# Four more products with w_out in three passes, and a new order of all steps

## The chip, the cores and the metric

The kernel runs on one core of a Trainium2 chip. The metric is the time of one execution on the device in microseconds (us), as the median of several runs.

## The reference

Attention with a causal mask feeds two matrix stages. Cut to what matters:

```python
q, k, v: (2, 12, 448, 64)
scores = where(triu, -1e9, (q @ k.T) / 8)
x = softmax(scores) @ v            # as 896 tokens x 768
h = x @ moe_w_in                   # 768 x 2048
x = (maximum(h, 0) ** 2) @ moe_w_out                       # 2048 x 768
h = maximum(maximum(x @ w1, x @ w2), x @ w3)               # 768 x 768 each
out = h @ w_out                    # 896 x 768, float32
```

## The kernel before

All tokens and weights are kept transposed on 128 partitions. The twelve pairs of heads go through attention one by one (`Pair`): score matmuls in plain float32 (step s), the masked minimum on VectorE (m), the exponential on ScalarE (e), the normalizing on GpSimd or VectorE (n), transposes on PE (g), their placing by ScalarE or VectorE (h) and the weighing with v on PE (w).

The four matrix stages each use a fast scheme for 2 x 2 blocks with seven products M1 to M7 in place of eight. `First` is x @ w_in in eight column pairs f0 to f7, `Second` is the product with moe_w_out in eight blocks o0 to o7 of its inner dimension, `Third` is the three products with w1, w2, w3 (h0 to h8), and the code at the end is the product with w_out.

A product is made in three passes over split operands: each operand is split in a rounded part (hi) and the rest (lo), both of a type that PE takes in one pass, and the product is hi*hi + hi*lo + lo*hi. For one product of `First`, `Second` or `Third` that is nine matmuls of 448 columns; in some of them one is cut into two of 224 columns (`matmul_in_parts`). The weights' split is `Quarter`: H.name casts 128x384 on ScalarE, H'.name on GpSimd, and L.name subtracts on VectorE. The result lies in one of five buffers (`RING`), which come free when PE has read them. In `Second` the moving operand is split as well: XH.name on ScalarE, XL.name on VectorE, 128x448 each; it lies in one of a pool of units. Steps S1 to S4 form sums of moving operands on VectorE, T1 to T4 sums of weights in place, T1, T3 and T4 by an accumulating DMA that GpSimd issues. C and J unpack a block of weights on ScalarE and VectorE, V steps carry results out of PSUM.

`FULL` names products of `Second` that are not split: M1 of blocks 0 to 3 go through `run_full`, three matmuls in plain float32 each, straight from the loaded weights and the activations (line 852).

The order of all steps is a table, `ORDER`: the program is written step by step as it stands there, and every engine works through its instructions in that order and waits only for the data and buffers that they need. A quote after a step's letter names the other engine for it. Behind the table a fixed tail follows with the rest of the last stage.

Of the kernel before, what the change touches and what calls it, by code (L numbers as in the profile page):

```python
# [33 lines left out]
h2.1 m0.3 e3.2 s4.3 n3.1 e0.3 a0'.2 m1.3 s2.3 a2.2 a1'.2 r0.2 n6'.2 h0.1 xh.0 g1.1 h1.1 r2.2 m4.3
r1.2 n0'.2 g3.2 s6.3 n5.2 m5.3 m3.3 e4.3 s6.4 n2.2 m2.3 n4.2 n3.2 e5.3 m6.3 h3.2 e1.3 m6.4 wload
n1.2 g0.2 e6.3 a0'.3 g1.2 g2.2 s0.4 xl.0 e2.3 xf'.0 a2'.3 s2.4 m0.4 e3.3 m1.4 s4.4 r0.3 r2.3 m2.4
m3.4 s2.5 e2.4 a1'.3 r1.3 n6.3 n1'.3 n3.3 h0'.2 e3.4 m5.4 m4.4 e6.4 w0.1 w1.1 n4'.3 h2'.2 n2.3
w2.1 h1.2 a1'.4 w3.1 e5.4 e0.4 n0.3 n5.3 g1.3 r1.4 g2.3 g3.3 n3.4 e1.4 e4.4 h2.3 a2'.4 s6.5 h1'.3
g0.3 d3.1 w0.2 m2.5 w1.2 w2.2 e2.5 C.i0 h3.3 a0'.4 w3.2 r0.4 n5.4 m3.5 n2.4 r2.4 s4.5 m6.5 h0.3
# [18 lines left out]
M1b.f0 a1'.11 w0.9 C.i4 n1.10 4l.3 H.f0M6 d4.7 r1.11 n4'.10 w1.9 w2.9 a2.11 w3.9 M1c.f0 r0.11
M2a.f1 r2.11 M2b.f0 4h.7 h3.10 g2.10 h1.10 n5.11 M1b.f1 3l.5 2h.7 g0.10 n4.11 d3.9 n0.11 4l.7
n1'.11 1l.7 h2.10 h0.10 g2.11 T1.f1 n3'.11 g0.11 w0.10 V0.f0M1 h2.11 n6.11 T3.f0 J.i4 w1.10 w2.10  # L60
3h'.9 2l.7 w3.10 T4.f0 xh'.10 xl.10 H'.f0M7 T3.f1 n2.11 C.i5 h0.11 g3.11 g1.11 J.i5 h3.11 h1.11
M1c.f1 xf.10 L.f0M6 M2c.f0 w0.11 w1.11 w2.11 T2.f1 w3.11 M2b.f1 V0.f1M1 T4.f1 C.i7 d2.11 L.f0M7
M2c.f1 2h.11 2l.11 M6.f0 H.f2M2 H.f1M6 d1.11 L.f1M6 xh.11 V0.f0M6 1h'.11 H.f1M7 J.i7 more V0.f1M2
# [1176 lines left out]
```

## Time and profile before

| | us |
|---|---|
| median of three runs | 449.04 (448.46 to 449.26) |
| the profiled execution, its own time | 448.89 |
| its span, first to last instruction | 446.9 |
| PE busy in the span | 441.8 |
| VectorE busy | 392.2 |
| ScalarE busy | 294.8 |
| GpSimd busy | 130.3 |

The clock of TensorE was granted in full throughout (1.00 in every stretch). The span falls into the attention stage (up to about 88 us), `First` (to about 188), `Second` (from 180 to about 294, with `Third` beginning inside its end), `Third` (to about 407) and the rest. The time of the profiled execution is its span and about 2 us around it. PE's own busy share says little, since matmuls overlap each other in the records; more is read from when one group starts after the other.

### The profile page before, as it was taken

Reading aid. Unit: us, or ns where it says so; the run is one execution under the profiler, and the core shown is the slowest. Engines: PE = TensorE matmul, PEld = TensorE weight load, DVE = VectorE, ACT = ScalarE, POOL = GpSimd, SP = SyncE. Lnnn points to the kernel's source line nnn. Section 1 sums busy time; section 2 is a strip of 40 time slices with the busy share of each in tenths; the row PEclk is TensorE's granted clock in tenths of the full one; section 3 lists DMA queues with packets and bytes.
Section 4 is the critical chain, followed back from the end, with each engine's and each line's share of the span. In section 5 each row is a group of like instructions: output and inputs, shape, how many; then the busy total and the mean of one; then the engine's idle time right before and its main releaser. Section 6 shows DMA issues by size and latency. Waiting matters only on the chain.

```text
span 446.9 us, 7146 instructions
## 1 busy us (share of the span) xinstructions
PE 441.8 (99%) x2380; PEld 387.0 (87%) x2380; DVE 392.2 (88%) x847; ACT 294.8 (66%) x657; POOL 130.3 (29%) x212
## 2 busy tenths in 40 slices
PE   8999999999999999999999999999999999999996
PEld 5666667799999999789999999999999999999996
DVE  5899999998987789999999899999897778889963
ACT  5999999766685797977566795656454533542651
POOL 4666575422311112142654312210321012100000
PEclk9999999999999999999999999999999999999999
DMA  7383374456646454899596554304462440000114
GB/s 223 114 266 123 115 240 149 124 170 195 194 113 205 133 151 118 235 181 208 146 168 180 162 160 141 119 24 141 142 211 72 142 132 11 2 0 0 37 53 160
DMA packets 42853, 61.01 MB, mean 137 GB/s; under 512 B 2113, under 2 KB 35009, under 8 KB 42817
## 3 DMA queue, kind: packets, MB, share of 16 engines
q1 hardware_dynamic: 39072, 55.61, 40.2%
q0 software_dynamic: 3456, 4.72, 6.4%
q8 instruction: 19, 0.31, 0.3%
q10 hardware_dynamic: 288, 0.23, 0.2%
q14 instruction: 18, 0.14, 0.1%
HBM read 53.08 MB, written 2.75 MB: 125 GB/s over the span
## 4 chain that ended last, share of the span: by engine, by line
PE 94%; DVE 5%; issue 0%
PE ps L583 69%; PE ps L438 7%; PE ps L480 5%; PE ps L511 5%; PE ps L1027 5%; PE ps L852 2%; DVE piece L200 1%; DVE z L210 1%; DVE wd L210 1%; PE ps L1092 1%; DVE s L210 0%; DVE z2l L200 0%; DVE wol L200 0%; DVE half L200 0%; DVE warm L1087 0%
## 5 line engine op out<-in xcount | busy, mean ns | idle before, releaser
L583 PE MATMUL ps<-s,wq 128*128 128x448 f32 (+1 forms) x629 | 130.1, 361 | 0.0
L583 PEld LDWEIGHTS ps<-s,wq 128*128 128x128 f32 x629 | 115.5, 188 | 9.6 <-issue 0.7
L583 PE MATMUL ps<-a,wq 128*128 128x448 f32 x459 | 99.3, 367 | 0.0
L583 PE MATMUL ps<-x,wq 128*128 128x448 f32 (+1 forms) x481 | 96.5, 362 | 0.0
L583 PEld LDWEIGHTS ps<-x,wq 128*128 128x128 f32 x481 | 88.3, 188 | 7.5 <-issue 0.7
L583 PEld LDWEIGHTS ps<-a,wq 128*128 128x128 f32 x459 | 85.8, 188 | 7.2 <-issue 0.4
L287 POOL CAST wq<-wd 128x384 fp32r<-128x384 f32 x43 | 36.1, 842 | 115.1 <-PE ps L583 97.0
L271 DVE SCALAR_TENSOR_TENSOR wd<-wr,up 128x768 int32<-128x768 int32 x56 | 55.1, 984 | 8.0 <-ACT up L264 4.2
L200 DVE TENSOR_TENSOR wq<-wd,wq 128x384 fp32r<-128x384 f32 x95 | 52.7, 566 | 8.3 <-POOL wq L287 5.2
L261 ACT CAST up<-wr 128x768 f16<-128x768 bf16 x40 | 43.2, 1080 | 12.4 <-DVE wd L271 3.1
L287 POOL CAST wq<-wt 128x384 fp32r<-128x384 f32 x32 | 21.5, 673 | 93.0 <-PE ps L583 74.4
L200 DVE TENSOR_TENSOR wq<-wt,wq 128x384 fp32r<-128x384 f32 x68 | 38.1, 571 | 11.9 <-ACT wq L197 7.7
L457 ACT ACTIVATE pr<-pr,st 128x256 f32<-128x256 f32 (+3 forms) x84 | 43.9, 530 | 3.8 <-DVE st L449 3.2
L197 ACT CAST wq<-wd 128x384 fp32r<-128x384 f32 x52 | 26.7, 513 | 26.0 <-PE ps L583 21.3
L472 POOL TENSOR_SCALAR pr<-pr,st 128x384 f32<-128x384 f32 (+3 forms) x64 | 36.9, 589 | 13.3 <-DVE st L468 11.3
L449 DVE CUSTOM_DVE_ANT_0 pr<-ps,mask 128x128 f32<-128x128 f32 (+3 forms) x84 | 34.7, 442 | 4.8 <-PE ps L438 4.0
L616 ACT COPY s<-ps 128x448 f32<-128x448 f32 x38 | 19.9, 530 | 24.6 <-PE ps L583 24.6
L438 PE MATMUL ps<-k,q 64*128 64x128 f32 (+3 forms) x168 | 34.7, 448 | 0.0
L197 ACT CAST wq<-wt 128x384 fp32r<-128x384 f32 x36 | 18.4, 511 | 15.7 <-PE ps L583 15.3
L480 PEld LDWEIGHTS ps<-ident,pr 128*128 128x128 f32 x192 | 21.3, 141 | 6.2 <-issue 2.8
L480 PE MATMUL ps<-ident,pr 128*128 128x128 f32 x192 | 25.5, 277 | 0.0
L438 PEld LDWEIGHTS ps<-k,q 64*128 64x128 f32 (+1 forms) x168 | 17.8, 196 | 8.7 <-DVE st L449 4.0
(123 smaller groups left out, 642.3 us busy)
## 6 DMA issues: line engine op xcount, KB each, us to landing
wr<-in_moe_w_out SPq DMA_DIRECT2D x22, 768.0 KB, 4.5
wr<-in_moe_w SPq DMA_DIRECT2D x18, 768.0 KB, 4.4
wr<-in_moe_w_in SPq DMA_DIRECT2D x16, 768.0 KB, 4.9
v<-in_v SPq DMA_DIRECT2D x12, 256.0 KB, 4.6
wd<-wd POOLq DMA_DIRECT2D x16, 192.0 KB, 5.5
q<-in_q SPq DMA_DIRECT2D x11, 256.0 KB, 2.6
out<-s SPq DMA_DIRECT2D x14, 192.0 KB, 2.0
k<-in_k SPq DMA_DIRECT2D x11, 224.0 KB, 2.9
```

What stands on the lines that cost most here:

```text
L197: nc.scalar.copy(hi, src)
L200: nc.vector.tensor_tensor(out=lo, in0=src, in1=hi.bitcast(F32), op=SUB)
L261: copy(self.up.bitcast(FH)[:, :, 1::2], self.top)
L271: nc.vector.scalar_tensor_tensor(out=self.t.bitcast(I32), in0=self.rest, scalar=13, in1=self.up.bitcast(I32), op0=ALU.logical_shift_right, ...
L287: copy(self.t[:, 0], self.src())
L438: nc.tensor.matmul(sc[:, :keys[w]], self.n["q"][r, w // 2 * P:(w // 2 + 1) * P], self.n["k"][r, :keys[w]], start=True, stop=True,)
L449: nc.vector.tensor_tensor_reduce(out=self.pr[:, offs[u]:offs[u] + n], in0=self.sc[u][:, :n], in1=mask[:, mask.shape[1] - n:], scale=-SCALE ...
L457: nc.scalar.activation(sl, sl, ACTF.Exp, bias=self.st[:, 0, u:u + 1], scale=-1.0, accum_out=self.st[:, 1, u:u + 1],)
L472: engine.tensor_scalar(sl, sl, self.st[:, 2, u:u + 1], 1.0, op0=ALU.mult, op1=ALU.mult)
L480: nc.tensor.transpose(pt[:, i], self.pr[:, offs[u] + kc * P:offs[u] + (kc + 1) * P], shared["ident"])
L511: nc.tensor.matmul(self.pv[r, kc * P:], self.n["v"][:, kc, r], self.ph[:, h, at], start=kc == 0, stop=kc == NK - 1,)
L583: nc.tensor.matmul(acc[:, c], w, x[:, c], skip_group_check=True, **flags)
```

## The change

`FULL` becomes empty: the four plain products M1.o0 to M1.o3 are split like the others. For each of them four steps come into the table (XH, XL, H or H', L), 16 in all. The table is replaced by one from a new search, so that nearly every engine's order changes in places, and 143 of the old steps stand on another engine than before. The number of casts of weights on GpSimd goes from 78 to 87, on ScalarE from 93 to 88. Nothing else in the code changes.

```diff
-FULL = dict(M1=(0, 1, 2, 3))
+FULL = dict()
...
-s0.0 m0.0 s2.0 m1.0 s4.0 m2.0 e0.0 m3.0 s6.0 e1.0 e3.0 m4.0 m5.0 a2'.0 m6.0 e4.0 r2.0 n1.0 e5.0
+s0.0 m0.0 m1.0 s2.0 e1.0 e0.0 s4.0 m2.0 m3.0 m4.0 e3.0 m5.0 s6.0 s6.1 e4.0 e5.0 a2'.0 m6.0 e6.0
```

On PE at the place of the first plain product, before (ps are PSUM banks, a22 and s4 operands of `First`, g activations, wd loaded weights, wq split weights):

```order
L583 MATMUL ps1_69<-a22_579,wq_1987 128x448 x3
L583 MATMUL ps1_69<-a22_903,wq_1987 128x448 x3
L583 MATMUL ps1_69<-a22_1175,wq_1987 128x448 x3
L852 MATMUL ps6_74<-g0_1244,wd_1764 128x448
L852 MATMUL ps7_75<-g0_1244,wd_1764 128x448
L852 MATMUL ps0_68<-g0_1244,wd_1764 128x448
L583 MATMUL ps4_72<-s4_690,wq_2034 128x448 x3
L583 MATMUL ps4_72<-s4_1035,wq_2034 128x448 x3
L583 MATMUL ps4_72<-s4_1264,wq_2034 128x448 x3
L852 MATMUL ps6_74<-g2_1191,wd_1620 128x448
```

and now (x is a split moving operand):

```order
L585 MATMUL ps1_69<-s3_465,wq_2007 128x448 x3
L585 MATMUL ps1_69<-s3_776,wq_2007 128x448 x3
L585 MATMUL ps1_69<-s3_1198,wq_2007 128x448 x3
L585 MATMUL ps6_74<-x_1559,wq_1963 128x448 x3
L585 MATMUL ps7_75<-x_1559,wq_1963 128x448
L585 MATMUL ps7_75<-x_1559,wq_1963 128x224 x2
L585 MATMUL ps7_75<-x_1559,wq_1963 128x448
L585 MATMUL ps0_68<-x_1559,wq_1963 128x448 x3
L585 MATMUL ps4_72<-s4_803,wq_2035 128x448 x3
L585 MATMUL ps4_72<-s4_1055,wq_2035 128x448 x3
L585 MATMUL ps4_72<-s4_1342,wq_2035 128x448 x3
```

The three plain matmuls of M1.o0 have become nine and one cut in two, from x and wq in place of g0 and wd, and M4.f7 stands behind M1.o2 now and M7.f7 ahead.

On VectorE at the same place, from the last output of `First`'s blocks 6 and 7 on, before:

```order
L210 TENSOR_TENSOR g15_2070<-ps5_73,s_2014 128x448
L271 SCALAR_TENSOR_TENSOR wd_2084<-wr_2028,up_64 128x768
L210 TENSOR_TENSOR s2_2088<-g9_1824,g8_1743 128x448
L210 TENSOR_TENSOR g10_1787<-g10_1787 128x448
L200 TENSOR_TENSOR wq_2094<-wd_1588,wq_2094 128x384
L271 SCALAR_TENSOR_TENSOR wd_2100<-wr_2048,up_64 128x768
L200 TENSOR_TENSOR x_2065<-g8_1743,x_2065 128x448
L200 TENSOR_TENSOR wq_2053<-wd_1661,wq_2053 128x384
L210 TENSOR_TENSOR g13_1999<-ps4_72,s_1889 128x448
L200 TENSOR_TENSOR wq_2067<-wd_1764,wq_2067 128x384
L200 TENSOR_TENSOR wq_2059<-wd_1753,wq_2059 128x384
L210 TENSOR_TENSOR g0_1244<-s2_1900,g0_1244 128x448
```

and now (x_1948 is the operand of M1.o3, wq_1986 and wq_2038 are the weights of M1.o1 and M1.o2; g0 is overwritten by S1 of block 0):

```order
L212 TENSOR_TENSOR g13_2063<-ps4_72,s_2020 128x448
L273 SCALAR_TENSOR_TENSOR wd_2067<-wr_1943,up_64 128x768
L202 TENSOR_TENSOR wq_2035<-wd_1476,wq_2035 128x384
L202 TENSOR_TENSOR x_1948<-g6_1534,x_1948 128x448
L202 TENSOR_TENSOR x_2053<-s2_1828,x_2053 128x448
L202 TENSOR_TENSOR wq_2076<-wd_1622,wq_2076 128x384
L212 TENSOR_TENSOR g0_1281<-s2_1828,g0_1281 128x448
L212 TENSOR_TENSOR g15_2106<-ps5_73,s_2073 128x448
L202 TENSOR_TENSOR wq_1986<-wd_1681,wq_1986 128x384
L202 TENSOR_TENSOR wq_2038<-wd_1774,wq_2038 128x384
L202 TENSOR_TENSOR wq_2110<-wd_1707,wq_2110 128x384
L212 TENSOR_TENSOR g2_1167<-s2_1828,g2_1167 128x448
```

Splits of the four products stand between the others, and the sums that overwrite g0 and g2 follow them.

On VectorE at the end of the table, the last row of each being the first of the fixed tail, before:

```order
L210 TENSOR_TENSOR s_4125<-ps6_74,s_4125 128x448
L210 TENSOR_TENSOR z5_3959<-z5_3959,s_4125 128x448
L200 TENSOR_TENSOR wol5_4222<-wd_4133,woh5_4155 128x768
L210 TENSOR_TENSOR z4_3963<-ps1_69,z4_3963 128x448
L200 TENSOR_TENSOR wol3_4227<-wd_3705,woh3_4051 128x768
L210 TENSOR_TENSOR z3_3681<-z3_3681 128x384
L210 TENSOR_TENSOR wd_3072<-wd_3072 128x384
```

and now:

```order
L212 TENSOR_TENSOR s_4081<-ps6_74,s_4081 128x448
L202 TENSOR_TENSOR wol5_4270<-wd_4157,woh5_4203 128x768
L212 TENSOR_TENSOR z4_3993<-ps1_69,z4_3993 128x448
L212 TENSOR_TENSOR z0_3396<-z3_3703,z0_3396 128x384
L212 TENSOR_TENSOR z5_4064<-z5_4064,s_4081 128x448
L212 TENSOR_TENSOR wd_3067<-wd_3067 128x384
```

One split of weights (wol3) stands earlier, and a maximum into z5 comes last.

## Rows read from the trace of the kernel before

**Rows 1.** The page: busy us (share of span) xinstructions; the chain's shares.
```profile
PE 441.8 (99%) x2380; PEld 387.0 (87%) x2380; DVE 392.2 (88%) x847; ACT 294.8 (66%) x657; POOL 130.3 (29%) x212
...
PE 94%; DVE 5%; issue 0%
```

**Rows 2.** Waits of PE: line, whom for, us, times, longest.
```profile
PE ps L1092 <- DVE warm L1087: 1.2, 1, 1.2
PE ps L1027 <- DVE s L210: 0.3, 1, 0.3
```

**Rows 3.** Windows: per stretch length, busy us (xinstructions) of five engines, clock, DMA.
```profile
8.48:87.78 79.30, 79.29 (x568) 54.43 (x567) 75.44 (x281) 75.25 (x232) 48.58 (x99) 1.00 0.52 161
87.78:180.45 92.67, 92.67 (x469) 86.04 (x465) 78.14 (x132) 67.63 (x134) 18.78 (x28) 1.00 0.56 163
...
194.64:406.70 212.06, 212.06 (x1067) 196.72 (x1066) 193.71 (x346) 118.77 (x220) 55.47 (x66) 1.00 0.44 121
```

**Rows 4.** The plain products' line: ns min/median/max, starts; who waited (us, times).
```profile
L852 PE MATMUL ps<-g,wd x24: 537/539/540, 180.4 to 194.6; 128*128 128x448 f32 x24
...
  POOL wd L207: 5.9, 2
```

**Rows 5.** Timeline of PE, 178 to 200: start, us, what.
```profile
178.62 1.99 PE L583 MATMUL ps<-a,wq 128*128 128x448 f32 x9
180.45 2.42 PE L852 MATMUL ps<-g,wd 128*128 128x448 f32 x6
...
184.55 2.42 PE L852 MATMUL ps<-g,wd 128*128 128x448 f32 x6
...
188.63 2.42 PE L852 MATMUL ps<-g,wd 128*128 128x448 f32 x6
```

**Rows 6.** Groups by form: xcount | busy us, mean ns | idle before.
```profile
L200 DVE TENSOR_TENSOR wq<-wd,wq 128x384 fp32r<-128x384 f32 x95 | 52.7, 566 | 8.3 <-POOL wq L287 5.2 <-ACT wq L197 2.7
...
L200 DVE TENSOR_TENSOR x<-g,x 128x448 fp32r<-128x448 f32 x36 | 22.9, 650 | 0.9 <-ACT x L197 0.9
...
L197 ACT CAST wq<-wd 128x384 fp32r<-128x384 f32 x52 | 26.7, 513 | 26.0 <-PE ps L583 21.3 <-DVE wq L200 1.3 <-POOL wq L287 1.2
...
L197 ACT CAST x<-g 128x448 fp32r<-128x448 f32 x36 | 19.5, 562 | 7.5 <-PE ps L583 5.2 <-DVE g L210 2.2
...
L287 POOL CAST wq<-wd 128x384 fp32r<-128x384 f32 x43 | 36.1, 842 | 115.1 <-PE ps L583 97.0 <-DVE g L210 6.8 <-ACT s L197 4.8
```

**Rows 7.** Windows around the change of stage, as in rows 3.
```profile
130.00:160.00 30.00, 30.00 (x152) 27.86 (x151) 20.13 (x34) 19.54 (x42) 4.55 (x8) 1.00 0.45 132
160.00:230.00 70.00, 70.00 (x334) 61.17 (x333) 66.17 (x117) 53.47 (x113) 25.88 (x31) 1.00 0.75 182
230.00:340.00 110.00, 110.00 (x555) 102.10 (x554) 105.27 (x187) 68.19 (x125) 28.12 (x30) 1.00 0.48 143
```

**Rows 8.** Waits from 88 to 407 on ScalarE and VectorE, as rows 2.
```profile
ACT wq L197 <- PE ps L583: 36.6, 34, 3.0
...
DVE wq L200 <- ACT wq L197: 10.9, 10, 2.1
DVE wq L200 <- POOL wq L287: 9.2, 14, 2.2
```

**Rows 9.** GpSimd's casts of one kind: ns min/median/max, first and last start.
```profile
L287 POOL CAST wq<-wd x43: 502/542/3647, 38.5 to 379.8; 128x384 fp32r<-128x384 f32 x43
```

**Rows 10.** Timelines of PE at 424 and of VectorE from 407.
```profile
424.35 1.28 PE L1027 MATMUL ps<-piece 128*128 128x384 f32 x6 [0.31 <-DVE s L210]
...
407.32 0.62 DVE L210 TENSOR_TENSOR z<-ps,z 128x448 f32<-128x448 f32 x1
407.86 0.94 DVE L200 TENSOR_TENSOR wol<-wd,woh 128x768 fp32r<-128x768 f32 x1
408.72 0.55 DVE L210 TENSOR_TENSOR z<-z 128x384 f32<-128x384 f32 x1
409.19 0.55 DVE L210 TENSOR_TENSOR wd<-wd 128x384 f32<-128x384 f32 x1
```

More of the change, by code (lines that the diff above doesn't have):

```diff
@@ L34 @@
[L34 to L39, printed above, removed]
@@ L58 @@
[L58 to L63, printed above, removed]
@@ L142 @@
[L142 to L143 removed]
+s0.0 m0.0 m1.0 s2.0 e1.0 e0.0 s4.0 m2.0 m3.0 m4.0 e3.0 m5.0 s6.0 s6.1 e4.0 e5.0 a2'.0 m6.0 e6.0
+r2.0 e2.0 m6.1 s0.1 m0.1 m1.1 a0.0 n1.0 r0.0 a1'.0 n4.0 e6.1 n6'.0 n5.0 s4.1 s2.1 m4.1 e1.1 n0'.0
+r1.0 m2.1 m3.1 g3.0 m5.1 n2.0 e4.1 n3.0 h3.0 e3.1 s6.2 e0.1 g0.0 m6.2 g2.0 g1.0 h0.0 s0.2 h2.0
+h1'.0 m0.2 a2'.1 r2.1 m1.2 s4.2 s2.2 w0.0 e2.1 e5.1 e6.2 w1.0 a1.1 e1.2 w2.0 n1.1 m4.2 r1.1 e4.2
@@ new lines @@
+d1.11 2h.11 C.i7 H.f1M7 2l.11 more V0.f1M2 H.f0M5 1h'.11 J.i7 M6.f0 1l.11 M6.f1 3h'.9 H'.f0M3
+V0.f0M6 H.f1M5 xh'.11 xl.11 3l.9 M7.f0 L.f1M5 T3.f2 V1.f1M2 L.f0M5 V0.f1M6 C.i11 J.i11 H.f2M1
+L.f2M1 M5.f1 T4.f0 M5.f0 T4.f1 C.i6 L.f1M7 L.f0M3 H.f1M4 M7.f1 V0.f0M7 H.f0M4 V0.f1M7 J.i6 L.f0M4
+T1.f2 V0.f0M2 V1.f1M7 L.f1M4 T1.f3 V1.f0M7 M4.f0 T3.f3 C.i12 V0.f0M4 H.f1M3 d4.11 M4.f1 H'.f3M1
+M1.f2 L.f3M1 J.i12 V0.f1M4 M1.f3 4h.11 T2.f2 H'.f2M2 V1.f0M2 4l.11 V2.f0M2 V0.f2M1 H'.f3M2 T2.f3
+L.f2M2 L.f1M3 C.i10 M3.f0 J.i10 H'.f3M6 M2.f2 M3.f1 V0.f3M1 H.f2M6 V0.f0M3 L.f3M2 H'.f3M5 T1.f5
@@ new lines @@
+XH.o7M5 L.o6M5 T3.o6 XL.o6M5 XL.o1M7 XH.o5M7 XL.o7M5 XH.o1M3 H.o0M7 XL.o4M7 M5.o6 T4.o6 S4.o7
+M5.o7 J.b1 V2.oM6 H.o2M7 H'.o1M7 T4.o7 V0.oM6 L.o0M7 H'.o0M4 V1.oM6 T4.o3 L.o1M7 T3.o7 L.o0M4
+T4.o5 C.b0 H.o5M7 L.o2M7 XL.o3M7 XH.o7M3 M7.o0 J.b0 XL.o5M7 XH.o3M4 M7.o1 M7.o2 XH.o0M4 XL.o0M3
+H'.o4M7 XL.o0M4 H'.o3M7 L.o3M7 M7.o3 C.a1 XH.o6M4 L.o4M7 H.o6M7 J.a1 XL.o1M3 C.c1 T3.h1 L.o5M7
+XL.o7M3 XL.o7M7 H.o7M7 M7.o4 T1.h1 L.o7M7 H.o3M4 M7.o5 H'.o2M4 L.o6M7 J.c1 M7.o6 M7.o7 XL.o6M4
+XH.o4M4 T2.h1 H.o1M4 XL.o3M4 V0.oM7 T1.h0 XL.o4M4 XH.o2M4 V1.oM7 V2.oM7 L.o3M4 L.o1M4 XH.o2M3
@@ new lines @@
+V0.h4M4 M4.h5 L.h6M1 M1.h6 M5.h5 C.c5 H.h7M1 L.h7M1 WH.1 L.h6M6 V0.h6M1 H'.h6M4 WL.1 M6.h6 V2.h4M7
+V2.h2M7 V0.h5M4 M1.h7 H'.h6M2 H'.h5M2 L.h6M2 T4.h7 V0.h6M6 V1.h5M7 M3.h5 J.c5 T1.h8 H'.h6M7
+H'.h8M1 L.h6M7 V0.h4M3 L.h5M2 L.h6M4 M7.h6 V1.h2M3 H.h6M5 M2.h5 H'.h8M5 M2.h6 V0.h6M7 T2.h8
+V1.h4M3 C.z4 J.z4 H.h8M6 T3.h8 V0.h5M2 M4.h6 L.h6M5 H'.h7M5 V0.h6M4 Z3.1 L.h8M6 V0.h6M2 L.h8M1
+V0.h7M1 V0.h5M3 ZH.0 M5.h6 M1.h8 V0.h8M1 L.h7M5 H'.h6M3 ZH.30 H'.h7M2 M5.h7 H.h7M6 ZL.0 L.h6M3
+WL.0 M6.h8 Z3.2 ZH.2 WH.4 L.h7M2 V1.h6M7 H.h8M2 M2.h7 L.h7M6 ZH.1 V0.h8M6 H'.h8M7 M6.h7 WL.2
@@ L144 @@
+H'.h7M3 ZL.30 WH.3 V2.h5M7 L.h8M2 M2.h8 V0.h7M2 L.h8M7 WL.4 V0.h7M6 T4.h8 H'.h7M7 M3.h6 ZL.1 C.z5
+V1.h5M3 ZL.2 M.0 M7.h8 V0.h6M3 L.h8M5 J.z5 V0.h8M2 L.h7M7 ZH.31 ZL.31 L.h7M3 M7.h7 ZH.l ZL.l M.2
+H'.h7M4 M5.h8 V.0 V0.h7M7 L.h7M4 WH.5 V0.h8M7 H.h8M3 V1.h7M7 WL.3 V2.h7M7 H'.h8M4 L.h8M3 Z2.l
+M3.h7 V1.h8M7 V0.h7M3 M4.h7 M3.h8 V1.h7M3 Z4.l V0.h7M4 L.h8M4 M4.h8 M.1 V2.h8M7 V0.h8M3 WL.5
+V0.h8M4 V.1 Z1.l V.2 V1.h8M3
 """
```

192 lines of the change are left out of this document (90 added, 102 removed).

## The prediction, made before the result was known

> **What bounds the kernel now.** I read the page's busy shares first: TensorE is busy 99% of the span and holds 94% of the chain that ended last [rows 1]. A busy PE need not be a PE at its peak, so the list of PE's waits comes next: it holds 1.5 us in all, 1.2 of them before the first instruction and 0.3 near the end [rows 2]. Then the stretches [rows 3]. From 87.78 to 180.45 us, 92.67 us, PE runs 464 three-pass matmuls by the program (the row counts 5 more that overlap the edges); 16 of them are half as wide, so 456 whole ones at 0.203 us each. The same pace fills the rest up to 406.7. So behind the attention stage every microsecond is a matmul's, and a matmul less is time less, as long as the operands keep coming. Before 87.78 the picture is another: VectorE and ScalarE are both busy 75.4 and 75.3 of 79.3 us there, so three engines are level, and no one of them alone sets the end.
>
> **Fewer passes on PE.** The four plain products are 12 matmuls, recorded as 24 halves between 180.4 and 194.6 [rows 4]. Their cost must be read with what follows, since the end of one shows as a late start of the next [rows 5]: from 180.45 to 184.55, 4.10 us, PE does one plain product (3 matmuls) and one three-pass product (9). Nine three-pass matmuls take 180.45 - 178.62 = 1.83 us there. So a plain product is 4.10 - 1.83 = 2.27 us, and its replacement 1.83: 0.44 less, four times 1.76. The product of block 0 gets one matmul split in two halves, about 0.01 more. I take **-1.75 us**. The 0.54 us in [rows 4] is the duration of a record that overlaps its neighbours, so it isn't used. The next pair of products, from 184.55 to 188.63, takes 4.08; by that the sum is -1.67, and the bounds are -1.6 and -1.8.
>
> The row says 0.203 us for a matmul of 448 columns. [...]
>
> **More work on the feeding engines.** Each of the four products now needs its moving operand split (XH on ScalarE, XL on VectorE) and its weights split (H on ScalarE or GpSimd, L on VectorE). By group means [rows 6]: XL 0.650 and L 0.566, four of each 4.9 us on VectorE; means include overlap with the next instruction, and by steps from start to start (0.54 for 448 columns, 0.47 for 384 [rows 10]) it is 4.0 us. On ScalarE four XH at 0.562, 2.2 us, come in, and since the new order has 88 H steps there and 87 on GpSimd (93 and 78 before), five H at 0.513, 2.6 us, go: nothing net. GpSimd gets nine casts more, 7.6 us at 0.842, and was busy 55 of 212 us in the last big stretch [rows 3].
>
> What hides the 4.0 us? VectorE idles 9.9 us from 130 to 160, 3.8 from 160 to 230 and 4.7 from 230 to 340 [rows 7]. Most of the new steps stand around the place of the four products, which lies in the tightest of these. The plain products gave VectorE a breather there: 9 us of PE time that asked nothing of it. On the other hand the new order table has XL of blocks 1 to 3 ahead of the first of the four products and each L one to four products ahead of its own, and the totals fit: 4.0 against 18.4 of idle time up to 340. Two waits also go: T1 and S1 of a block overwrite what the plain product read, so they stood behind PE, and GpSimd lost 5.9 us to that [rows 4]; now they need only the splits to be done. I take **0** on the path, with 0 to +4.0 as bounds.
>
> **The order of the attention stage.** Up to the last placing step of pair 11 the new order moves 6 normalizing steps from GpSimd to VectorE, and on balance 3 placing steps and 2 casts from VectorE to ScalarE. The same 30 matmuls of the first stage (10 blocks of 3) stand ahead of the last weighing step in both orders, and the first twenty PE steps are the same. By group means the totals up to there differ by some tenths of a microsecond on VectorE and half a microsecond on ScalarE. Neither order can beat the three engines' work: each of VectorE and ScalarE has 3.9 to 4.1 us idle in this stage [rows 3]. I take **0**, with a third of that idle time, 1.3, as a gain at best and half of it, 2.0, as a loss.
>
> **The end.** The 0.31 us wait of PE at 424.35 [rows 10] is the one wait behind the attention. VectorE works without a break from 408.7 to 425, so its start there decides. Before the fixed tail begins at 409.19 it takes, from 407.32, the maximum with the last product (0.54), a weights split (0.86) and a subtraction (0.47): 1.87. In the new order it takes that maximum, an addition of the subtraction's size and one more maximum (0.54): 1.55, with one split fewer. That is 0.3 earlier: **-0.3**, bounds -0.3 (the wait is gone) and +0.3.
>
> **Sum**, against the profiled execution's 448.89 us (span 446.9; the median of the three runs is 449.04, 0.03% away): 448.89 - 1.75 - 0.3 = **446.8 us**, 0.5% faster. This measurement tells 0.2%, 0.9 us, from no change.
>
> **Rivals.**
> 1. *VectorE becomes the bound at the change of stage.* For: VectorE waits 20.1 us on the hi-casts, because casts wait for a ring of five weight buffers that PE frees (36.6 us on ScalarE alone) [rows 8]; such idle time can't be filled by other work of the same queue. From 160 to 230 it idles 3.8 us, less than the 4.0 that come in. If what is added lands there whole, PE waits for it: 446.8 + 4.0 = 450.8, **slower** by 0.4%. It decides when the splits are not done before the stretch from about 175 us, so that the first of PE's waits for a split shows between 180 and 200. Against: from 230 to 340 VectorE is busy 96% [rows 7] with a split for every product, and PE has no wait.
> 2. *The attention stage is ordered less well* (2.0 us, above): 448.8, no change. For: all three engines are level there, so any misplaced step shows. Against: the same totals, the same PE order at the start.
> 3. *GpSimd casts come late.* The same cast takes 0.502 to 3.647 us [rows 9], and VectorE waited 9.2 us in 14 waits for the 78 of them [rows 8]: 0.118 each. Nine more would add 1.06, if PE sees all of it: 446.8 + 1.1 = 447.9, at the edge of what can be told. [...]
> 4. *The new order is better in the attention stage* by the 1.3 us above: 445.5.
>
> That the products don't change isn't among them: the order of the new program has no row of the plain product's line left.
>
> **How the numbers follow.** The forecast has 0.58, with a range of its own from 446.0 to 447.9; rival 1 0.12, rival 2 0.14, rival 3 0.08 (half of it on either side of 448.1), rival 4 0.08. Faster: 0.58 + 0.08 + 0.04 = 0.70; same: 0.14 + 0.04 = 0.18; slower 0.12. The range from 445.5 to 449.2 takes in the forecast, rivals 2 and 3 with a little above them, and half of rival 4, which lies around its lower end; it leaves out rival 1 and the other half, 0.16.
>
> **What would show it.** Right: no plain matmul in the profile; from the end of attention to the last big product PE without waits at 0.203 us; that stretch 1.7 us shorter; its start within 1 us of 87.78; no wait of PE behind 420. Wrong: PE waits on VectorE or on casts between 180 and 230 (rival 1 or 3, told apart by whether VectorE was working or waiting for a GpSimd cast), or a later end of attention (rival 2).

## The result, and the profile after

The changed kernel takes 455.17 us (median of 4 runs, 454.05 to 455.46) against 448.81 for the kernel before: a ratio of 1.0137, 95% interval 1.0116 to 1.0157. It is **slower by 1.4%**, 6.4 us; forecast were 446.8 us, 0.5% faster, and a range up to 449.2. The profiled execution (454.99 us, span 453.2) has these lines where [rows 1] stood before: busy us (share) xinstructions, and the chain that ended last by engine.

```profile
PE 444.1 (98%) x2393; PEld 389.5 (86%) x2393; DVE 399.3 (88%) x860; ACT 294.4 (65%) x658; POOL 144.0 (32%) x214
...
PE 74%; DVE 14%; issue 4%; POOL 3%; ACT 2%; DMA 1%; POOLq 0%; ACTq 0%; DVEq 0%
```

The chain tells it at once. TensorE held 94% of it before and now 74%, VectorE 14%: behind the attention stage there are now places where TensorE is not what is late. Its list of waits, against [rows 2]:

```profile
PE ps L585 <- DVE wq L202: 3.7, 5, 1.8
PE ps L1094 <- DVE warm L1089: 1.2, 1, 1.2
PE ps L482 <- ACT ph L505: 0.2, 1, 0.2
```

The wait of 0.3 us at the end is gone, as forecast, and five waits for the low half of a weight (wq on VectorE) are new. (Lines stand two further down in the changed kernel: L583 is L585, L200 is L202, L287 is L289.) The same two stretches as in [rows 3], from the first matmul to the end of attention and from there to the last big product, the second with a mean clock of 0.99:

```profile
8.48:88.81 80.33, 79.78 (x562) 54.10 (x560) 75.18 (x282) 73.93 (x230) 46.73 (x93) 1.00 0.49 159
88.81:413.54 324.73, 320.97 (x1599) 295.00 (x1595) 292.07 (x508) 198.68 (x379) 94.17 (x106) 0.99 0.47 134
```

The attention stage ends 1.03 us later (87.78 before). The stretch behind it took 406.70 - 87.78 = 318.92 us and takes 324.73 now: 5.8 longer, where TensorE's term asked for 1.75 less. So 7.6 us were lost in there, and the waits of TensorE in its timeline lie at 221, 251, 258, 293 and 392 us, with smaller late starts at 184 and 270. Two of them (start us, us, what, [idle before <- whom for]):

```profile
251.34 5.79 PE L585 MATMUL ps<-x,wq 128*128 128x448 f32 x28 [0.57 <-DVE wq L202]
257.94 2.33 PE L585 MATMUL ps<-x,wq 128*128 128x448 f32 x10 [0.82 <-DVE wq L202]
```

A listed wait leaves out the first 0.16 us of a pause, in which the matmul before is still recorded as busy: a record lasts 0.365 us here, and without a wait the next starts 0.203 us after it. From start to start, over the pause and the matmul behind it and against 0.203 us each, TensorE loses 0.26 us at 184, 0.53 at 221, 0.84 at 251, 1.09 at 258, 0.26 at 270, 0.46 at 293 and 2.08 at 392 us: 5.5 us.

The largest is this one. TensorE's timeline and behind it VectorE's:

```profile
390.10 0.56 PE L585 MATMUL ps<-a,wq 128*128 128x448 f32 x2
392.48 2.14 PE L585 MATMUL ps<-a,wq 128*128 128x448 f32 x7 [1.82 <-DVE wq L202]
```

```profile
385.32 0.56 DVE L202 TENSOR_TENSOR wq<-wt,wq 128x384 fp32r<-128x384 f32 x1
389.69 0.96 DVE L202 TENSOR_TENSOR wol<-wd,woh 128x768 fp32r<-128x768 f32 x1 [3.81 <-PE ps L585]
390.56 0.86 DVE L202 TENSOR_TENSOR half<-z,half 128x384 fp32r<-128x384 f32 x1
391.34 0.61 DVE L212 TENSOR_TENSOR z<-z,s 128x448 f32<-128x448 f32 x1
391.88 0.54 DVE L202 TENSOR_TENSOR wq<-wd,wq 128x384 fp32r<-128x384 f32 x1
```

VectorE stood idle for 3.81 us in front of `wol` and waited for TensorE; the split that TensorE wants, L.h8M2, is three steps further back in VectorE's queue. `wol` is the step WL.2. It takes a buffer that `drop` gives back at M6.h8, the last block of the stage. In the old order M6.h7 ran ahead of M6.h8; in the new one it runs behind it, still reads that buffer, and WL.2 has to wait until it is through. And the windows of TensorE (length, busy us, granted clock, DMA) show a second price:

```profile
392.00:393.50 1.50, 1.02 (x5) 0.99 0.00 0
393.50:396.90 3.40, 3.40 (x11) 0.50 0.00 0
396.90:404.00 7.10, 7.10 (x38) 1.00 0.01 2
```

For 3.4 us the granted clock is half (0.50). Eight matmuls take 0.373 us from start to start there instead of 0.203, and those at the edges a little more too: another 1.5 us, and with it 7.0 of the 7.6 us are found. This price isn't paid every time: of the four runs of the changed kernel two have a mean granted clock of 0.994 and 0.995, this one among them, and two have 1.000. So the median of 455.17 us holds it only in part.

The waits at 251, 258 and 293 us were put down to GpSimd next. Its casts of weights (ns min/median/max), against [rows 9]:

```profile
L289 POOL CAST wq<-wd x48: 500/674/4509, 41.9 to 390.3; 128x384 fp32r<-128x384 f32 x48
```

In the page's groups their mean is 1045 ns, 842 before [rows 6]. Seven casts took 1.6 us or more between 230 and 320 us, and all seven were ScalarE's in the old order. One of them on GpSimd, and beside it VectorE:

```profile
283.86 4.42 POOL L289 CAST wq<-wd 128x384 fp32r<-128x384 f32 x2 [3.22 <-DVE wq L202]
```

```profile
286.37 0.55 DVE L202 TENSOR_TENSOR wq<-wd,wq 128x384 fp32r<-128x384 f32 x1
286.84 0.62 DVE L202 TENSOR_TENSOR x<-g,x 128x448 fp32r<-128x448 f32 x1
288.31 0.56 DVE L202 TENSOR_TENSOR wq<-wd,wq 128x384 fp32r<-128x384 f32 x1 [0.85 <-POOL wq L289]
```

The first of the two casts ran from 283.86 to 287.82, 3.97 us. VectorE worked without a pause until 287.46 and then waited for it. The cast ended 0.37 us after VectorE had stopped.

### The profile page after: what moved, and what is told of

Its sections match the earlier page's. It is cut to its first block, busy times and chain, and to the rows that moved or that the text cites. A ratio compares the mean times of both kernels' runs of the same rounds, so it can differ in the third digit from the quotient of the medians.

```text
span 453.2 us, 7186 instructions
## 1 busy us (share of the span) xinstructions
PE 444.1 (98%) x2393; PEld 389.5 (86%) x2393; DVE 399.3 (88%) x860; ACT 294.4 (65%) x658; POOL 144.0 (32%) x214
## 4 chain that ended last, share of the span: by engine, by line
PE 74%; DVE 14%; issue 4%; POOL 3%; ACT 2%; DMA 1%; POOLq 0%; ACTq 0%; DVEq 0%
PE ps L585 56%; PE ps L1029 7%; PE ps L440 5%; PE ps L482 3%; DVE wq L202 3%; DVE pr L451 2%; PE ps L513 2%; DVE wd L273 2%; POOL wq L289 2%; DMA wr<-in_moe_w 1%; PE ps L1132 1%; POOL wd L209 1%; DVE y L212 1%; DVE s L202 1%; DVE x L202 1%
## 5 line engine op out<-in xcount | busy, mean ns | idle before, releaser
L585 PE MATMUL ps<-s,wq 128*128 128x448 f32 (+1 forms) x629 | 130.7, 363 | 0.1
L585 PEld LDWEIGHTS ps<-s,wq 128*128 128x128 f32 x629 | 116.5, 190 | 9.7 <-issue 0.4
L585 PE MATMUL ps<-x,wq 128*128 128x448 f32 (+1 forms) x518 | 104.7, 362 | 1.8 <-DVE wq L202 1.8
L585 PEld LDWEIGHTS ps<-x,wq 128*128 128x128 f32 x518 | 94.7, 188 | 11.1 <-DVE wq L202 3.3
L585 PE MATMUL ps<-a,wq 128*128 128x448 f32 x459 | 100.3, 368 | 1.8 <-DVE wq L202 1.8
L585 PEld LDWEIGHTS ps<-a,wq 128*128 128x128 f32 x459 | 85.7, 188 | 9.4 <-DVE wq L202 2.6
L289 POOL CAST wq<-wd 128x384 fp32r<-128x384 f32 x48 | 49.8, 1045 | 92.9 <-PE ps L585 66.8
L273 DVE SCALAR_TENSOR_TENSOR wd<-wr,up 128x768 int32<-128x768 int32 x56 | 55.7, 995 | 8.0 <-ACT up L263 6.8
L202 DVE TENSOR_TENSOR wq<-wd,wq 128x384 fp32r<-128x384 f32 x99 | 55.2, 569 | 7.0 <-POOL wq L289 4.7
L289 POOL CAST wq<-wt 128x384 fp32r<-128x384 f32 x36 | 26.3, 732 | 106.2 <-PE ps L585 90.9
L459 ACT ACTIVATE pr<-pr,st 128x128 f32<-128x128 f32 (+3 forms) x84 | 44.2, 536 | 3.9 <-DVE st L451 3.8
L202 DVE TENSOR_TENSOR wq<-wt,wq 128x384 fp32r<-128x384 f32 x68 | 38.7, 576 | 7.8 <-POOL wq L289 7.4
L199 ACT CAST wq<-wt 128x384 fp32r<-128x384 f32 x32 | 16.2, 511 | 30.1 <-PE ps L585 27.0
L474 POOL TENSOR_SCALAR pr<-pr,st 128x384 f32<-128x384 f32 (+3 forms) x58 | 31.7, 559 | 11.6 <-DVE st L470 10.9
L440 PE MATMUL ps<-k,q 64*128 64x384 f32 (+3 forms) x168 | 34.1, 436 | 0.1
L199 ACT CAST x<-g 128x448 fp32r<-128x448 f32 x40 | 22.2, 563 | 12.4 <-PE ps L585 11.2
```

The source lines that it names most:

```text
L199: nc.scalar.copy(hi, src)
L202: nc.vector.tensor_tensor(out=lo, in0=src, in1=hi.bitcast(F32), op=SUB)
L273: nc.vector.scalar_tensor_tensor(out=self.t.bitcast(I32), in0=self.rest, scalar=13, in1=self.up.bitcast(I32), op0=ALU.logical_shift_right, ...
L289: copy(self.t[:, 0], self.src())
L440: nc.tensor.matmul(sc[:, :keys[w]], self.n["q"][r, w // 2 * P:(w // 2 + 1) * P], self.n["k"][r, :keys[w]], start=True, stop=True,)
L459: nc.scalar.activation(sl, sl, ACTF.Exp, bias=self.st[:, 0, u:u + 1], scale=-1.0, accum_out=self.st[:, 1, u:u + 1],)
```

## The experiments

Theory: TensorE's -1.75 us is there, but single steps of the new order make TensorE wait. Rivals: the 4.9 us of VectorE work that the change adds is what costs; or a sum of small things that no step explains.

### The casts back on ScalarE

Seven steps, which stand apart in the table, change their engine:

```diff
-H'.o1M7 H'.o4M7 H'.o4M4 H'.h1M6 H'.o2M3 H'.o6M3 H'.h3M1
+H.o1M7 H.o4M7 H.o4M4 H.h1M6 H.o2M3 H.o6M3 H.h3M1
```

> The changed kernel with seven high halves (o1M7, o4M7, o4M4, h1M6, o2M3, o6M3, h3M1) cast by ScalarE again, as before, where GpSimd took 1.66 to 4.51 us for each; their places in the order are the same. Theory: these casts start the chains that end in TensorE's waits at 251, 258 and 293 us, 0.84 + 1.09 + 0.46 = 2.4 us; they go, 455.2 - 2.4 = 452.8 us (452.2 to 453.8). Rival: VectorE is full from 160 to 300 us with or without them, and the waits are its queue: 454.7 us or more.

Measured 452.84 us, ratio 1.0083 (1.0062 to 1.0103): 2.4 us less, against the list of waits above:

```profile
PE ps L585 <- DVE wq L202: 2.4, 3, 1.8
```

TensorE's waits at 251 and 293 us and the late start at 270 are gone, 1.6 us together by their starts; that at 221 stays. These chains began at GpSimd, and VectorE's load alone does not make those waits. The wait at 258 us is 0.45 us here and 1.1 in the changed kernel, but f3_casts_and_wol below, which has the casts on ScalarE too, shows 1.3 us there again: it isn't the casts'. The 2.4 us is the theory's number partly by luck, since the two medians differ in the low clock as well: only one of the four runs, the profiled one, has a mean clock below 0.998 here (0.995). Between the runs without it the difference is 2.1 us, two runs against three.

### WL.2 alone, and with the casts

```diff
-M6.h7 WL.2 H'.h7M3 ZL.30 WH.3 V2.h5M7 L.h8M2
+M6.h7 H'.h7M3 ZL.30 WH.3 V2.h5M7 L.h8M2 WL.2
```

> The changed kernel with one step moved: WL.2 (the low half of a block of w_o, on VectorE) goes from behind M6.h7 to behind L.h8M2, three VectorE steps later; nothing else. Theory: WL.2 takes a buffer that is given back at M6.h8, which now stands ahead of M6.h7; M6.h7 still reads it, so VectorE stands idle for 3.8 us in front of WL.2, L.h8M2 comes 2.3 us late and TensorE waits 2.08 us in front of M2.h8, and then runs 3.41 us at a granted clock of 0.5. With WL.2 behind L.h8M2 the wait and the low clock both go: 2.08 + about 1.6 us, so 455.2 - 3.7 = 451.5 us (450.8 to 452.3). Rival: VectorE is so full there that the time saved is only spent at the next split; then under 1 us goes and the time is 454.2 us or more.

Measured 453.76 us (1.0102), about 1.5 us less and not 3.7. A part of the 3.7 was never in the median: it counts 1.6 us for the low clock, which two of the four runs of the changed kernel don't show. The wait and the low clock at 392 us are gone (the four runs' mean clocks are 0.998 to 1.000), but `wol` is now late itself and the products of the last stage, which read it and the z halves behind it in the queue, wait 0.78 us at 397 and 0.56 at 400. The truth lay between theory and rival: VectorE's lost 2.6 us there have to be filled with work, not only moved.

```diff
-M6.h7 WL.2 H'.h7M3
+M6.h7 H'.h7M3
...
-L.h8M2 M2.h8 V0.h7M2 L.h8M7 WL.4 V0.h7M6 T4.h8
+L.h8M2 M2.h8 V0.h7M2 L.h8M7 T4.h8 WL.2 WL.4 V0.h7M6
```

> The changed kernel with the seven casts on ScalarE again, as in e4_casts_back, and WL.2 moved, this time behind T4.h8 (which itself goes ahead of V0.h7M6), so that VectorE has four instructions to do until M6.h7 is through. Theory: 452.84 us of e4_casts_back less the wait of 1.97 us and the low clock's 1.4 to 1.6 us at 391 us, with 0 to 0.8 us given back at the products of the last stage: 449.3 to 450.3 us. Rival (the waits at the end belong to a VectorE that is full there too): what is saved at 391 us is waited for behind, as it partly was in e1_wl2_later, 451 us or more.

Measured 451.36 us (1.0057 with 1.0039 to 1.0075), 1.2 us under the casts alone by the ratios. That misses the theory's 449.3 to 450.3 us and lies in the rival's range, but not for the rival's reason: in its profile TensorE waits only 0.25 us at 397 us, and the clock stays at 1.00 from the first matmul to the end of the products. The sum subtracted the low clock from a median that hardly held it: three of the four runs of e4_casts_back have a mean clock of 1.000. And the wait at 257.6 us, 0.45 us in the profile with the casts alone, is 1.3 us here. Up to 390 us the two kernels have the same steps, so this is a difference between two executions. ScalarE's timeline there:

```profile
250.56 0.51 ACT L199 CAST wq<-wd 128x384 fp32r<-128x384 f32 x1 [0.50 <-PE ps L585]
254.97 1.07 ACT L263 CAST up<-wr 128x768 f16<-128x768 bf16 x1 [3.90 <-DMA wr<-in_moe_w]
255.90 0.92 ACT L199 CAST wq<-wd 128x384 fp32r<-128x384 f32 x2
```

ScalarE stands 3.9 us in front of C.c1, whose weights are still on their way; it stood 3.1 us there with the casts alone and 4.2 in the changed kernel. Both orders have one join between C.c1 and the unpacking before it (a join starts the load after the next). But in the old order H.o7M7 came ahead of C.c1; the new one put H.o7M7, which had all it needed, behind it.

### That one step, and the attention stage

```diff
-J.a1 XL.o1M3 C.c1 T3.h1 L.o5M7 XL.o7M3 XL.o7M7 H.o7M7 M7.o4 T1.h1 L.o7M7 H.o3M4
+J.a1 XL.o1M3 T3.h1 L.o5M7 XL.o7M3 XL.o7M7 H.o7M7 M7.o4 T1.h1 L.o7M7 H.o3M4 C.c1
```

> The kernel of f3_casts_and_wol with one ScalarE step moved: C.c1, which waits 3.9 us for its weights' DMA at 255 us with the cast H.o7M7 and others queued behind it, goes behind H.o7M7 and H.o3M4. Theory (the wait of TensorE at 257.6 us, 1.42 us, is ScalarE's order): it goes, 451.4 - 1.4 = 450.0 us (449.6 to 450.5). Rival (VectorE and the DMA hold TensorE there whatever ScalarE's order): under 0.4 us gained.

```diff
-s0.0 m0.0 m1.0 s2.0 e1.0 e0.0 s4.0 m2.0 m3.0 m4.0 e3.0
+s0.0 m0.0 s2.0 m1.0 s4.0 m2.0 e0.0 m3.0 s6.0 e1.0 e3.0
...
```

> The kernel of f3_casts_and_wol with the first 656 steps, up to M4.f0 of the first product stage, in the order and on the engines of the kernel before; behind them all other steps in the order of f3_casts_and_wol. Theory (the new order of the attention stage costs 1.0 to 1.4 us): the last of TensorE's attention matmuls starts at 87.5 to 88.0 us instead of 88.8, and the time is 451.4 - 1.0 to - 1.4 = 450.0 to 450.4 us. Rival (what comes late at the end of the attention stage is hidden by slack behind it, or the seam costs as much): within 0.4 us of 451.4.

Measured 449.81 us for the step (1.0025, 1.0013 to 1.0037) and 449.65 us for the old attention stage (1.0016, 1.0006 to 1.0027): by the ratios 1.4 and 1.8 us less than f3_casts_and_wol. In the profile with the step moved ScalarE doesn't wait in front of C.c1, and TensorE isn't late at 258 us. The last attention matmul starts at 86.8 to 88.0 us in nine profiles with the old order in front (87.6 in the kernel before, 86.8 in this one), and at 88.5 to 90.0 in nine with the new one, so this loss is no chance of one execution; the medians of the two sets are 1.5 us apart. Which step of the stage makes it isn't shown.

### All of it together

```diff
-XL.o1M4 V1.oM2 L.o3M6
+V1.oM2 L.o3M6
-XH.o7M3 M7.o0 J.b0 XL.o5M7 XH.o3M4 M7.o1 M7.o2 XH.o0M4 XL.o0M3 H.o4M7 XL.o0M4
+XH.o7M3 M7.o0 J.b0 XL.o5M7 XH.o3M4 M7.o1 M7.o2 XH.o0M4 XL.o0M3 H.o4M7 XL.o0M4 XL.o1M4
...
-L.f2M1 L.f0M3 V1.f1M7 L.f1M4
+L.f1M4 L.f2M1 L.f0M3 V1.f1M7
...
-J.z5 V0.h8M2 L.h7M7
+L.h7M7 J.z5 V0.h8M2
```

> The kernel of h2_old_attention with C.c1 behind H.o7M7 and H.o3M4 (as in h3_later_up_cast) and three VectorE steps moved where TensorE still waits: XL.o1M4 (wanted at 258 us) from in front of L.o3M6 to behind XL.o0M4, L.f1M4 ahead of L.f2M1, L.h7M7 ahead of J.z5. Theory (the losses are single steps of the order, and all are found): h2_old_attention's 449.65 us less its waits of 0.40 us at 255 us, 0.42 at 220 us, 0.45 at 102 us and 0.26 at 394 us, 448.1 us (447.4 to 448.8), 0.2% under the kernel before or a little more. Rival (each moved step is waited for elsewhere, since VectorE is 94 to 99% busy from 160 to 300 us): 449.2 us or more.

Measured **446.91 us** (7 runs, 446.27 to 448.02) against 448.69: ratio 0.9965, 0.9952 to 0.9977. This kernel beats both. It is also 1.2 us under its own forecast of 448.1. That one took the waits from the profile of h2_old_attention, the fastest of its ten runs (448.12 us), and subtracted them from the median (449.65), so it probably counted too little; no run shows this. The waits of TensorE, and the two stretches:

```profile
PE ps L1094 <- DVE warm L1089: 1.2, 1, 1.2
PE ps L513 <- DMA v<-in_v: 0.7, 1, 0.7
```

```profile
8.48:88.08 79.60, 78.74 (x562) 54.06 (x560) 75.14 (x278) 74.72 (x231) 49.60 (x98) 1.00 0.51 160
88.08:405.69 317.61, 317.51 (x1598) 294.31 (x1595) 290.48 (x507) 201.34 (x386) 78.57 (x100) 1.00 0.49 137
```

From the end of attention on TensorE has no listed wait, and the stretch is 318.92 - 317.61 = 1.3 us shorter than before. The largest late start left in it is 0.26 us at 183 us.

### Is it VectorE's added work?

> The changed kernel without the eight VectorE steps that the change adds (L and XL of o0M1 to o3M1): all three passes of these four products read the high halves, so TensorE does the same matmuls at the same places, and only their low parts are missing from the result. If the added VectorE work is all that costs, the time is that of the kernel before less TensorE's term, 448.8 - 1.75 = 447.0 us. If the new order is all that costs, nothing goes: 455 us. Theory (both): the waits at 183 and 221 us (0.9 us) go, those behind slow GpSimd casts (2.4 us) shrink by up to 1 us, the wait with the low clock at 392 us (3.7 us) and the 1.0 to 1.4 us of the attention stage stay: 452.8 to 454.3 us.

```diff
-self.acc(n, m), q.t[:, ew, m], x[:, ex],
+self.acc(n, m), q.t[:, ew * (n != "M1" or j > 3), m], x[:, ex * (n != "M1" or j > 3)],
```

Measured 454.76 us (1.0134, 1.0118 to 1.0151), 0.4 less than the changed kernel, within both intervals.

```profile
PE ps L585 <- DVE wq L202: 4.3, 6, 1.8
```

The waits at 221, 252, 259, 294 and 393 us are all there; only the late start of 0.3 us at 184 us is gone. So in the changed kernel the added work costs nothing that the times can tell; the order costs.

In the next kernel a step with a + in front issues its namesake's VectorE instruction again.

```diff
-XL.o4M1
+XL.o4M1 +XL.o4M1
...
-L.o4M1
+L.o4M1 +L.o4M1
...
```

> The kernel before, with eight VectorE instructions issued twice: the low halves L.o4M1 to L.o7M1 and XL.o4M1 to XL.o7M1, at 183 to 203 us, write the same values to the same place again. That is 4 x 0.57 + 4 x 0.65 = 4.9 us of VectorE work, as much as the change adds and at the same place, with nothing taken from TensorE and the order unchanged. Theory (VectorE is the second bound from 160 to 340 us: of 160 to 230 us it has 3.8 us idle, and those lie in front of waits it cannot use): TensorE waits 2 to 4.5 us for low halves between 190 and 260 us, 450.8 to 453.3 us. Rival (the term of the prediction: there is room beside TensorE): 449.3 us or less.

Measured 452.28 us (1.0079), 3.5 us more, with waits of TensorE for halves from 196 to 215 us:

```profile
PE ps L583 <- DVE wq L200: 1.4, 3, 0.8
...
PE ps L583 <- DVE x L200: 0.7, 1, 0.7
```

This is no contradiction. Put at this place into an order that is left as it is, the same work costs 0.7 us for each 1 us; planned for, it costs next to nothing. The last kernel above, k1_all_mended, carries all of it. Its windows, against [rows 7] (VectorE is the third of the busy times):

```profile
130.00:160.00 30.00, 30.00 (x151) 27.86 (x151) 25.33 (x44) 22.49 (x47) 7.58 (x11) 1.00 0.61 180
160.00:230.00 70.00, 69.90 (x354) 64.41 (x353) 68.00 (x119) 55.87 (x117) 25.00 (x33) 1.00 0.72 169
230.00:340.00 110.00, 110.00 (x555) 102.13 (x554) 104.11 (x188) 69.58 (x129) 21.09 (x24) 1.00 0.49 145
```

5.2 us more between 130 and 160, 1.8 more up to 230: the new order moved splits forward into the idle time of the earlier stage.

### The order without the splitting

```diff
-FULL = dict()
+FULL = dict(M1=(0, 1, 2, 3))
...
-XH.o0M1
...
-XL.o0M1
...
-H'.o0M1 L.o0M1
...
```

> The changed kernel's order with M1.o0 to M1.o3 plain float32 again and their sixteen steps left out: the order without the splitting. Theory (the order is what costs): TensorE pays 1.75 us more for the four products, the waits at 221, 251, 258, 293 and 392 us mostly stay, since what makes them is order: 455 to 457.5 us. Rival (VectorE's 4.9 us of added work is what costs): with it gone the waits at 221 to 293 us, 3.2 us together, go too, and some of the chain behind: 455.2 + 1.75 - 3.2 or more = 453.7 us or less.

Measured 462.17 us. Four steps that overwrite what the plain products read (T1 of blocks 1 and 3, S1 of blocks 1 and 2) stood ahead of them here, so the products were formed from other values and TensorE waited for those steps; the run doesn't answer the question.

```diff
-T1.o1 M3.f7 XH.o3M2 H.o1M2 S1.o1 V0.f6M3 M1.o1
+M3.f7 XH.o3M2 H.o1M2 V0.f6M3 M1.o1 T1.o1 S1.o1
...
```

> The changed kernel's order with M1.o0 to M1.o3 plain float32 again, their sixteen steps left out, and the steps T1.o1, T1.o3, S1.o1 and S1.o2, which overwrite what these products read, put behind them. Theory (the order costs, and VectorE's added work on top): the added work of 4.9 us is gone from a VectorE that is full from 160 to 300 us, so the waits of TensorE between 183 and 225 us (0.9 us) go, those of the slow GpSimd casts (2.4 us) shrink, the wait and the low clock at 392 us (3.7 us) stay, and the four products cost 1.75 us more: 453 to 455.5 us, 4 to 6.5 us over the kernel before. Rival (the added work is the whole cost): within 1 us of the kernel before, 448.8 us, since without it the order is as good as the old one.

Measured 462.94 us, far over both. With the plain products GpSimd waits for TensorE before it may overwrite the weights (T1), and VectorE for GpSimd's DMA: 11.5 us in one wait of GpSimd,

```profile
  PE ps L854: 11.5, 1
```

and TensorE stands 3.4 us at 211 us. This way the order and the splitting can't be taken apart; g1_after_no_lows and k1_all_mended do it.

### The splitting in the old order

The sixteen steps were put into the old order by hand.

```diff
-FULL = dict(M1=(0, 1, 2, 3))
+FULL = dict()
...
-J.o0r L.f7M4 XH.o3M2 H'.o3M2
+L.f7M4 L.o0M1 J.o0r XH.o3M2 XH.o2M1
...
```

> The kernel before with the splitting alone: M1.o0 to M1.o3 in three passes, their sixteen steps put into the old order by hand around 165 to 190 us; three splits of later operands (o0M7, o4M6, o0M6, o1M6) and the high halves of the M2 ones moved behind them so that buffers come round in the order of use; everything else in the old order. Theory (TensorE's term holds where the order leaves room): 448.8 - 1.75 = 447.1 us, up to 448.3 if one of the moved steps comes late by some tenths. Rival (VectorE becomes the bound at the change of stage, whatever the order): first waits of TensorE for a low half between 178 and 205 us, 1 to 4 us in all: 448.3 to 451 us.

Measured 450.21 us (1.0028, 1.0018 to 1.0039), slower than before by 1.3 us, with waits of 1.15 us at 211 us and of 0.2 to 0.5 at 212 to 250. That is in the rival's range, though its waits were to come between 178 and 205 us. Three tries to mend it:

```diff
-XL.o5M2 M1.o6 V2.f6M3 L.o5M2 S3.o6 S4.o2 M1.o7 H.o7M2 T1.o4 T2.o3 XH.o6M2 T3.o3
+XL.o5M2 M1.o6 V2.f6M3 L.o5M2 M1.o7 H.o7M2 T1.o4 XH.o6M2
...
```

> The kernel of e3_split_alone with VectorE's steps spread better: S3.o0, S3.o1, S2.o0 and S2.o1 go ahead of 160 us, where VectorE waits for ScalarE; S4.o0 to S4.o4, S3.o6, T2.o3, T3.o3 and L.o0M6 go behind 212 us. Theory (VectorE is the bound only because of how the work lies; 2.4 us of idle time ahead of 160 us can be used): the wait of 1.15 us at 211 us and some of those of 0.2 to 0.5 us at 222 to 250 us go, 447.5 to 449.0 us, and with that under the kernel before. Rival (from 165 to 340 us VectorE is at its limit whatever lies where): 449.8 us or more, the wait only moved.

(The edit of the next is that of g1_after_no_lows.)

> The kernel of e3_split_alone (the splitting in the old order) without the eight added VectorE steps, in the same way: three passes over the high halves in the four products, their low parts missing from the result. Theory (f2_before_double: 4.9 us of VectorE work there costs 3.5 us): without it TensorE's term shows in full, 448.75 - 1.75 = 447.0 us (446.6 to 447.9, since a step that was moved by hand can still be late by some tenths). Rival (what costs in e3_split_alone is the moved order or the added casts on ScalarE, not VectorE's work): 449 us or more.

```diff
-dve(self.g(j, 0, 0), self.s2[j], self.g(j, 0, 0), ADD)
+more(self.g(j, 0, 0), self.s2[j])
```

> The kernel of e3_split_alone with the eight sums S1.o0 to S1.o7 (128x448, g += s2, 0.6 us each on VectorE, at 185 to 230 us) done by accumulating DMAs that GpSimd issues, as T1, T3 and T4 already are. That takes as much from VectorE, 4.9 us, as the splitting adds. Theory (VectorE's work is the bound): the waits of 1.15 us at 211 us and of 0.2 to 0.5 us behind it go, 447.0 to 448.5 us, under the kernel before. Rival (the load comes back in another queue: eight more issues of about 0.85 us on GpSimd, in front of its casts, and transfers that come late): waits for GpSimd's casts between 190 and 240 us, 449 us or more.

Measured 452.33 (1.0079), 449.84 (1.0025) and 450.96 us (1.0050). Work pushed behind 212 us came due at 220 to 229 us, in waits of 1.0, 1.0 and 1.5 us; the sums by DMA made TensorE wait at 205 to 213 us, 2.5 us in all; and even without VectorE's added work waits of 0.2 to 0.7 us stay, 2.0 in all. All three lie in their rivals' ranges. Leaving out VectorE's added work takes off 0.4 us, within the noise, so in this kernel that work isn't the main cost either. In that run, from 175 to 185 us, ScalarE (fourth) is the full engine and VectorE has room:

```profile
175.00:185.00 10.00, 10.00 (x52) 9.28 (x51) 7.32 (x12) 10.00 (x22) 0.66 (x1) 1.00 0.69 177
```

```diff
-H.f6M4 H.o0M1
+H.f6M4 H'.o0M1
...
-XH.o7M2 XH.o0M6 S4.o4 XH.o5M6 XH.o5M2 H.o6M1
+XH.o7M2 S4.o4 XH.o5M2 H.o6M1
...
```

> The kernel of e3_split_alone with H.o0M1, H.o1M1 and H.o2M1 on GpSimd instead of ScalarE, the casts XH.o0M6 and XH.o5M6 behind H.o7M1 and so no longer in front of H.o6M1, S3.o0, S3.o1, S2.o0 and S2.o1 ahead of 160 us, S3.o6 and L.o0M6 behind L.o7M2, S4.o2 behind XL.o3M6, and XL.o3M3 and XL.o2M4 behind L.o0M4. Theory (in g2_split_no_lows ScalarE was 10.00 of 10 us busy at 175 to 185 us and VectorE 7.32: the added casts are ScalarE's, and VectorE waits for them): the wait of 1.15 us at 211 us and that of 0.52 us at 249.9 us go or halve, 448.2 to 449.3 us. Rival (VectorE's sum of work decides, as in f4_split_alone_2): new waits of 1 us or more at 215 to 235 us, 450.2 us or more.

Measured 450.13 us (1.0026): the wait at 211 us went, one of 1.1 us came at 226 and one of 0.55 at 284. A step moved by hand is waited for elsewhere; which engine is short there I can't say from these runs. The sums by DMA in the mended new order (below) didn't pay either.

The edit is that of g3_split_sums_by_dma.

> The kernel of f3_casts_and_wol (the new order, mended in two places) with S1.o0 to S1.o7 by accumulating DMAs. Theory: of its waits of TensorE (0.26 at 184 us, 0.5 at 221 us, 1.4 at 257.6 us, 0.36 at 396.6 us) the first two and some of the third go, 451.4 - 0.8 to - 2 = 449.4 to 450.6 us; the attention stage keeps it above the kernel before. Rival: GpSimd's queue is the longer one there, waits for its casts come in their place, 451 us or more.

Measured 454.29 us (1.0126), 2.9 more than without: waits of 1.5 us at 191, 0.8 at 197 and 2.2 at 260, the rival's result.

## Why the prediction was wrong

- **TensorE's term (-1.75 us)** was right. The changed kernel's matmuls run at 0.203 us wherever they don't wait and the clock is at 1.00, and with the waits mended the stretch behind the attention is 1.3 us shorter, with some 0.5 us of late starts left in it. (The 1.6 to 1.8 us of the whole kernel are something else: they hold 0.5 us from the end, too, and 0.3 lost up to the end of the attention.)
- **VectorE's added work (0 on the path)** was right for this order to some tenths: 0.4 us by g1_after_no_lows, within the noise, and 0.26 us at 183 us in k1_all_mended; the rest went where the idle time of [rows 7] was. Rival 1, the case that ended slower, was the wrong mechanism: its mark, the first wait of some size between 180 and 200, is 0.3 us at 184 us, and that wait alone goes without the added work.
- **The end (-0.3)** was right in its mechanism: no wait behind 420. From the last big product to the end it is 39.7 us, 40.2 before, 0.5 less.
- **The attention stage (0, at worst +2.0)** was mis-sized within its bounds: +1.0 by the profile, 1.8 by the run with the old order. This is rival 2's mechanism. Its list of moved steps also leaves out five small ones (L466 of the changed kernel, 0.24 us each on VectorE) that went from GpSimd to VectorE; whether they matter isn't shown.
- **The step that failed** is the sentence that behind the attention stage a matmul less is time less, "as long as the operands keep coming". I costed what the change adds and took the rest of the new order as neutral, because totals of idle time fit. But 143 old steps had changed engines and nearly every engine's order had changed in places, and a total says nothing of a queue. No term stood for that, and it lost 7.6 us. By the profile 1.6 of them are the late starts at 251, 270 and 293 us, which go with the seven casts; 1.1 at 258, which go with C.c1; 2.1 at 392 and 1.5 of the low clock, which go with WL.2; and 0.8 at 184 and 221. By the medians the mends are worth 2.4 (casts), 1.4 (C.c1) and 1.2 to 1.5 us (WL.2); these don't add up with the profile's to the tenth, since the low clock and the landing of C.c1's weights differ from run to run. The order of the new table, without any time, shows two of these places: M6.h8 ahead of M6.h7 with WL.2 behind, and C.c1, which waits on a load, ahead of H.o7M7.
- **Rival 3 (late GpSimd casts, +1.06)** was the right mechanism with the wrong size. It took the mean wait of 0.118 us for nine more casts. The price sits in a few: seven of 1.7 to 4.5 us, which together cost 1.6 us by the profile and 2.4 by the medians.
- **The chances** treated the rivals as one or the other. They were one cause, an order that is worse in several places, and came together: attention +1, casts +2.4, one ScalarE step +1.4, one buffer +1.2.

## What to carry to other kernels

Where a change comes with a new order of all steps, the order is the change: cost it as such, and give it a loss of its own, since a kernel without waits has only places to lose. For each buffer that the last reader frees, look which reader is last in the new order; for each step that waits on a DMA, look what stands behind it on its engine. And added work that costs 0.7 us per 1 us at one place of a fixed order can be nearly free in another order, so a test that adds work to the old order doesn't give the price in the new one. Before a price is taken from one profile, see whether the other runs paid it: the low clock was in two runs of four.
